# Turning the filter round with plain products into 64-row halves: one change to a long-convolution and mixer kernel

## The chip, the cores and the metric

The kernel runs on one core of one Trainium2 chip. The time is the device time of one execution in microseconds, and the profile is one execution recorded by the hardware profiler. The engines are TensorE (PE, with its weight loads as PEld), VectorE (DVE), ScalarE (ACT), GpSimd (POOL) and SyncE (SP), whose queue issues nearly all transfers.

## The reference

Two branches read the same input `q` (2048 tokens of 640 channels, bf16) and are mixed by a gate per token:

```
g = sigmoid((q * gate_w).sum(-1))
# branch A: a gated long convolution
k_shift[t] = sum over 4 taps of k[t - j] * shift_k[:, j]
kv = k_shift * v
y  = causal convolution of kv with ssm_k (640 x 2048), by FFTs of length 4096, + kv * ssm_D
a  = q * y
# branch B: a mixer block
h  = gelu(layernorm(q) @ w1); its four channel quarters shifted by +1, -1, +2, -2 tokens; hs = h @ w2
x1 = q + hs
b  = x1 + gelu(layernorm(x1) @ w3) @ w4
out = g * a + (1 - g) * b
```

## The kernel before

**The layout.** A token is n*32 + g*16 + s. The row (partition) of a tile is 64*g + n, and the sixteen values of s are sixteen slots of the free dimension. All loads of `q`, `k` and `v` come in this way: rows 0 to 63 hold g = 0, rows 64 to 127 hold g = 1. This is called the signal's row order here.

**Branch B.** The normalised input is transposed on PE in pairs of slots (`tr1`, L609; copied out by `ev1` and, for the ends, `evh`), multiplied by `w1` with the shifts (`w1`, L689 and L693), put through gelu (`g1`, ACT L706), multiplied by `w2` (`w2`, L715) and added to `q` (`x1`, DVE L722). The second norm (`nm2`) and a transposing DMA (`dt2`, L808) lead to `w3` (L817), gelu (`g2`, ACT L824) and `w4` (L833, L842).

**Branch A.** The convolution is an FFT in two steps of products with tables of sines (`TRIG`). `kv` is made on DVE in four groups of eight instructions (L878, L882, L886). Step 1 takes 16 slots of the filter (`s1h`, L911) and of the signal (`s1x`, L913), is copied out of PSUM (`e1h`, `e1x`, into FS) and written to DRAM (`wF`, L943). Step 2 (`s2`, L965) reads that back after every step 1 is written; then come a product of spectra on DVE (L980), the way back (`s3`, L993), another trip through DRAM (`wG`, `rG`), and the last step (`s4`, L1031), which meets branch B on DVE (`yq`, `ad`, `ax`, `fo`).

**The filter.** `ssm_k` is stored by channel, so it has to be turned: five blocks SK of 128 channels by 2048 times. `trh` (L859) uses PE's transposing mode, 16 blocks of 128x128 for each of the five, into a bf16 PSUM tile of 2048 columns; `evt` (L387 on ACT, L389 on DVE) copies it to HT. A transpose of columns s, s + 16, s + 32 ... puts time 16*q + s into row q, so even rows hold g = 0 and odd rows g = 1. This isn't the signal's row order. Step 1 must sum over the 64 rows of each g apart, so the kernel keeps a second table BM: zeroed on POOL (`bz`, L499), then the sines written to every other row by two DMAs (`bm`, L503). Step 1 of the filter then multiplies all 128 rows, half of them with zeros; that of the signal uses rows 0 to 63 and 64 to 127 as two separate 64-row tiles of the array.

**The order.** Everything is a list of tasks (`Plan.add`), each with the engine it may run on and an estimated duration. The string ORDER fixes the sequence and the engine of each task. `Plan.place` walks it with the estimates, only to choose buffers and the number of filler products (L255, products with zeros that keep PE running while it waits early on). The eight PSUM banks are the pool U; most tasks take a pair of banks. A bank is held until its copy has ended.

Of the kernel before, what the change touches and what calls it, by code (L numbers as in the profile page):

```python
# [12 lines left out]
BF16 = mybir.dt.bfloat16  # L13
# [24 lines left out]
41 0 23 5 29 94v 6 7 9 3 19 11 17 4 25 1 2 31 32 15 18 8 10 63v 12 13 14 26 27 87v 61a 85a 64 62 95v 104v 65v 28 42 88  # L38
86 393 24 44 96 209 43 210 55a 66v 89v 67 395 56 68a 58a 53v 54 97v 34 90a 30 399 396v 400v 57v 91 397 40 394a 93a 98
59 99v 100v 92v 60v 101 103v 143 147 16 20p 33 149 398a 102a 77a 145 79v 21 45 150 80 391 71v 72 46 22 144 148 69v  # L40
392v 82v 74a 121 39 122 450 70 78 146 107a 73v 458 35 75 451v 401p 438 37 81v 76v 439a 151 83 113v 123 36 459a 38 456
152 457a 49 84v 108 114 454 452 115v 116 125 455a 453a 110v 129 117v 446 444 126 460 118v 403 404 405 124 127 447a 162
163 406 130 128 156 157 440 105a 441a 407 159 153 154 106 160 461 47 445a 402 131 158 109a 155 442 111 132 137 443a
112a 408 161 462 466 48 138 409 463a 448 134 135 468 215p 216 449 164 140 469a 467a 119 413 141 51 221p 165 470 410 50
411 120a 166 222 223v 464 465a 167 474 471a 173 475a 174 171 217a 480 168 476 187 191 481a 482 193 477a 172 473 192
188 412 414 218 483a 478 169 195 189 170 181 415 416 417 479a 472 418 419 421 422 182 178 179 485 196 194 190 486 423
488 219a 484 225a 489a 175 220 487a 492 176 493a 136 203 424 204 494 425 490 206 498 207 495a 200 201 491a 420 426 427
# [12 lines left out]
673 681 343 684 661 682a 680a 685a 344 674 686 687a 688 629 297 645 675a 689 676v 690 677 301 692v 691a 693 345 302  # L60
# [23 lines left out]
class Plan:  # L84
# [13 lines left out]
    def add(self, name, eng, dur, fn, r=(), w=(), use=(), acq=(), rel=(), roles=(), after=(), mode=None, nbytes=0):  # L98
# [3 lines left out]
        t.kept = None  # L102
        t.acq = [(a, 1, a == "U") if isinstance(a, str) else a for a in acq]
# [43 lines left out]
    def place(self, order):  # L147
# [6 lines left out]
        mode, bw, flying, self.kept = None, 0.0, [], None  # L154
        start, end = [None] * n, [None] * n
        for i in order:
# [34 lines left out]
            else:  # L191
                d = t.dur
# [17 lines left out]
                free[e] = end[i] = at + d  # L210
            for (o, p, k) in t.rel:
# [143 lines left out]
def build(env, nc, io):  # L355
    pl = Plan()
    add = pl.add
    for name, n in (("U", 8), ("xn", 4), ("hs", 2), ("x1nT0", 1), ("x1nT1", 1), ("h2", 2), ("FS", 2), ("FX", 5), ("XS", 2), ("HS", 2), ("PP", 2),
                    ("GX", 4), ("Q", 2), ("O", 2), ("V", 4)):
# [51 lines left out]
    add("ident", "POOL", 0.55, c_id, r=["iotb"], w=["ID"])  # L411
# [92 lines left out]
    add("bm", "SP", 1.08, c_bm, r=["TRIG"], w=["BM"], nbytes=P * 4096 * HALF, roles=("C0",))  # L504

# [6 lines left out]
    add("cjp", {"POOL": 3.2, "ACT": 2.3}, 0, lambda t: copy(t, env["VC"][0:1, 3, :, :],  # L512
# [106 lines left out]
    for s0 in pairs:  # L619
        nm = []  # L620
        for s in (s0, s0 + 1):
            st1[s] = add(f"st1.{s}", {"DVE": 1.26, "ACT": 1.73}, 0, lambda t, s=s: f_st1(t, s), r=[("x", s, 0), ("x", s, 1)],
                         w=[("MV", s)])
            add(f"rs1.{s}", "POOL", 0.85, lambda t, s=s: f_rs1(t, s), r=[("MV", s), "c0"], w=[("RS", s)])
        for s in (s0, s0 + 1):
# [7 lines left out]
            nm1[s] = add(f"nm1.{s}", {"DVE": 0.445, "ACT": 1.2}, 0, f_nm1, r=[("RS", s), ("x", s, 0), ("x", s, 1)],  # L633
# [10 lines left out]
        def f_ev1(t, s0=s0, tt=tt):  # L644
            copy(t, env["xnT"][:, s0 + 2:s0 + 4, :, :], tview(env.Ub(tt.buf["U"][0])))
        add(f"ev1.{s0}", {"ACT": 1.25, "DVE": 0.82}, 0, f_ev1, use=[tt], rel=[(tt, "U")], w=[("xnT", s0), ("xnT", s0 + 1)],
            roles=("xnT",))
        if s0 in (14, 0):
            h0 = 0 if s0 == 14 else 18

            def f_evh(t, s0=s0, tt=tt, h0=h0):
# [10 lines left out]
            add(f"evh.{s0}", {"DVE": 1.0, "ACT": 1.3}, 0, f_evh, use=[tt], rel=[(tt, "U")], w=[("xnT", a), ("xnT", a + 1)],  # L662
                roles=("xnT",))
# [130 lines left out]
    for c in range(4):  # L794
        nT, nP = None, f"x1nT{c % 2}"
        for s0 in (4 * c, 4 * c + 2):
            ss = (s0, s0 + 1)
            add(f"ve2.{s0}", {"DVE": 0.42, "POOL": 1.5}, 0, lambda t, s0=s0: f_ve2(t, s0), r=[("x", s, 0) for s in ss] + [("S2", s) for s in ss],
                w=[("v2", s0)])
            add(f"st2.{s0}", "POOL", 1.5, lambda t, s0=s0: f_st2(t, s0), r=[("v2", s0)] + [("x", s, 0) for s in ss],  # L800
# [53 lines left out]
    for cb in range(5):  # L854
        def trh(t, cb=cb):
            sk = env["SK"][:, cb, :].rearrange("c (q s) -> c q s", s=16)
            o = env.Ub(t.buf["U"][0])
            for i in range(16):
                nc.tensor.transpose(o[:, 128 * i:128 * i + 128], sk[:, :, i], env["ID"][:])  # L859
        t = add(f"trh.{cb}", "PE", 1.0, trh, r=["ID", ("SK", cb)], use=[fill], acq=("U",), mode="f", roles=("SK",))  # L860

        def evt(t_, cb=cb, t=t):
            copy(t_, env["HT"][:, :, 128 * cb:128 * cb + 128], env.Ub(t.buf["U"][0]).rearrange("p (s c) -> p s c", s=16))
        add(f"evt.{cb}", {"ACT": 1.86, "DVE": 1.23}, 0, evt, use=[t], rel=[(t, "U")], w=[("HT", cb)], after=("PRE",), roles=("HT",))
    add("dfold", {"DVE": 0.5, "POOL": 0.9}, 0, lambda t: (nc.vector if t.on == "DVE" else nc.gpsimd).tensor_tensor(out=env["HT"][0:1, 0, :], in0=env["HT"][0:1, 0, :],
                                                               in1=env.early("DR", [1, D], BF16), op=ALU.add),
        r=["DR"] + [("HT", cb) for cb in range(5)], w=["HT0"], roles=("HT", "C0"))
# [33 lines left out]
    def step1(which, order):  # L901
# [3 lines left out]
        def reads(s, cbs):  # L905
            return ["BM" if which == "h" else "TRIG"] + ([("HT", cb) for cb in cbs] + (["HT0"] if s == 0 else []) if which == "h" else [("kv", s)])
        roles = ("HT", "C0") if which == "h" else ("K",)

        def prod(out, s, c0, c1, g):
            if which == "h":  # L910
                nc.tensor.matmul(out, lhsT=BM()[:, g, 128 * s:128 * s + 128], rhs=src(s)[:, c0:c1], start=True, stop=True)  # L911
            else:
# [194 lines left out]
```

## Time and profile before

| what | value |
|---|---|
| time, median of 3 runs (lowest to highest) | 225.08 us (224.55 to 225.7) |
| the profiled execution: time, span | 227.05 us, 225.3 us |
| busy PE, DVE, ACT, POOL | 212.7, 189.3, 154.4, 45.8 us |
| instructions | 5381 |
| moved by DMA | 57.94 MB, mean 257 GB/s |
| granted TensorE clock | 1.000 |

The profiled execution's own time is 1.97 us above the median of the runs, and its span is 1.75 us below its time. Busy PE contains the filler products. Shares over the whole span hide the stages: up to about 40 us PE waits for loads, norms and copies; from then on it is nearly always at work.

### The profile page before, as it was taken

What the parts mean: (1) busy time and instruction counts of PE and PEld (TensorE: products, weight loads), DVE (VectorE), ACT (ScalarE), POOL (GpSimd) and SP (SyncE); (2) the same over time, 40 slices, a digit from 0 to 9 for tenths busy, and PEclk for the clock granted to TensorE, in tenths of its full rate; (3) what the DMA queues carried; (4) which work ended last, traced back from release to release, by engine and by line L of the source; (5) the groups of instructions that cost most, each with busy time, mean ns of one, the idle gap of its engine ahead of it and who ended that gap; (6) DMA issues with size and microseconds to landing.
All of it is one profiled execution on the core that took longest, in us unless ns stands there. A gap on an engine that the chain in (4) does not pass through costs nothing.

```text
span 225.3 us, 5381 instructions
## 1 busy us (share of the span) xinstructions
PE 212.7 (94%) x2161; PEld 106.4 (47%) x2178; DVE 189.3 (84%) x281; ACT 154.4 (69%) x225; POOL 45.8 (20%) x86
## 2 busy tenths in 40 slices
PE   3999889899999999999999999999999999999992
PEld 1576454466444444345543433334444555555561
DVE  7998896999999999997469989899857426989984
ACT  6998969799988999889658988888675002225000
POOL 7481532436200009930710000000000000000000
PEclk9999999999999999999999999999999999999999
DMA  6999999999999998979899989999992596988624
GB/s 193 281 308 232 220 237 238 327 233 327 349 240 287 241 272 252 379 270 270 193 367 311 373 154 285 316 304 309 247 255 88 185 374 209 281 250 249 203 64 116
DMA packets 39503, 57.94 MB, mean 257 GB/s; under 512 B 15027, under 2 KB 30645, under 8 KB 39478
## 3 DMA queue, kind: packets, MB, share of 16 engines
q1 hardware_dynamic: 39158, 57.27, 89.9%
q10 hardware_dynamic: 320, 0.33, 0.5%
q8 instruction: 17, 0.28, 0.5%
q14 instruction: 8, 0.07, 0.1%
HBM read 35.56 MB, written 18.36 MB: 239 GB/s over the span
## 4 chain that ended last, share of the span: by engine, by line
PE 63%; DMA 17%; DVE 12%; SPq 3%; issue 2%; ACT 1%; DVEq 0%
PE PS L817 18%; PE PS L833 17%; PE PS L715 9%; DMA x<-in_A_q_dram 7%; PE PS L965 5%; DMA W<-in_B_w_dram 4%; PE PS L689 4%; PE PS L993 4%; DMA SK<-in_A_ssm_k_dram 3%; DVE VC L878 3%; DVE VC L882 3%; DMA QO<-in_A_q_dram 2%; SPq L382 2%; PE PS L911 2%; PE PS L1031 1%
## 5 line engine op out<-in xcount | busy, mean ns | idle before, releaser
L824 ACT ACTIVATE h2T<-PS 128x512 bf16<-128x512 f32 x48 | 27.9, 605 | 27.3 <-PE PS L817 26.9
L833 PE MATMUL PS<-W,h2T 128*128 128x512 bf16 (+3 forms) x306 | 39.8, 298 | 0.3
L387 ACT CAST FS<-PS 128x1024 bf16<-128x1024 f32 x37 | 36.0, 1021 | 5.4 <-PE PS L913 3.5
L817 PEld LDWEIGHTS <-W 128*128 128x128 bf16 (+1 forms) x300 | 22.1, 103 | 29.4 <-issue 8.4
L833 PEld LDWEIGHTS <-h2T 128*128 128x128 bf16 (+1 forms) x312 | 22.4, 100 | 18.5 <-issue 1.6
L387 ACT CAST XH<-PS 128x1024 bf16<-128x1024 f32 x26 | 25.5, 1020 | 7.5 <-PE PS L965 7.4
L817 PE MATMUL PS<-x1nT,W 128*128 128x512 bf16 x120 | 28.5, 380 | 0.0
L817 PE MATMUL PS<-XB,W 128*64 128x512 bf16 (+1 forms) x180 | 28.5, 380 | 0.0
L980 DVE TENSOR_TENSOR PP<-XH 128x2048 bf16<-128x2048 bf16 x20 | 23.6, 1219 | 3.1 <-ACT XH L387 2.8
L878 DVE TENSOR_TENSOR VC<-K,VC 128x2560 bf16<-128x2560 bf16 x16 | 23.7, 1490 | 2.3 <-DMA W<-in_B_w_dram 2.1
L715 PE MATMUL PS<-W,hsT 128*128 128x128 bf16 (+1 forms) x155 | 23.5, 297 | 0.9 <-DMA W<-in_B_w_dram 0.6
L850 DVE TENSOR_TENSOR x<-PS,x 128x640 bf16<-128x640 f32 x12 | 9.8, 823 | 13.4 <-PE PS L833 13.2
L689 PE MATMUL PS<-xnT,W 128*128 128x512 bf16 x80 | 19.2, 379 | 0.1
L715 PEld LDWEIGHTS <-hsT 128*128 128x128 bf16 x160 | 12.8, 98 | 13.0 <-issue 1.1
L882 DVE TENSOR_TENSOR VC<-VC 128x2560 bf16<-128x2560 bf16 x12 | 17.9, 1489 | 0.3
L389 DVE CAST XH<-PS 128x1024 bf16<-128x1024 f32 x14 | 16.9, 1220 | 1.2 <-PE PS L965 1.1
L1037 DVE SCALAR_TENSOR_TENSOR W<-PS,GG,QO 128x640 bf16<-128x640 f32 x16 | 13.6, 877 | 2.4 <-PE PS L1031 1.9
L387 ACT CAST GS<-PS 128x1024 bf16<-128x1024 f32 x12 | 12.0, 1016 | 3.9 <-PE PS L993 3.9
L255 PE MATMUL PS<-C 128*128 128x512 bf16 x34 | 9.9, 434 | 3.8 <-DVE C L506 3.7
L842 PE MATMUL PS<-W,h2T 128*64 128x512 bf16 (+1 forms) x192 | 13.4, 299 | 0.0
L722 DVE SCALAR_TENSOR_TENSOR x<-PS,x 128x640 bf16<-128x640 f32 x16 | 12.8, 815 | 0.1
L965 PE MATMUL PS<-FX,TRIG 64*32 64x512 bf16 x320 | 12.4, 381 | 0.3 <-ACT GS L387 0.3
(115 smaller groups left out, 294.0 us busy)
## 6 DMA issues: line engine op xcount, KB each, us to landing
FH<-FS SPq DMA_DIRECT2D x8, 640.0 KB, 6.3
FXD<-FS SPq DMA_DIRECT2D x8, 640.0 KB, 5.0
FX<-FH SPq DMA_DIRECT2D x10, 512.0 KB, 6.0
FX<-FXD SPq DMA_DIRECT2D x10, 512.0 KB, 5.3
GX<-GD SPq DMA_DIRECT2D x8, 640.0 KB, 5.9
W<-in_B_w_dram SPq DMA_DIRECT2D x2, 1920.0 KB, 11.9
GD<-GS SPq DMA_DIRECT2D x8, 480.0 KB, 4.0
SK<-in_A_ssm_k_dram SPq DMA_DIRECT2D x5, 512.0 KB, 6.5
```

The lines of the kernel that those rows point to most:

```text
L387: nc.scalar.copy(out=out, in_=in_)
L389: (nc.vector if t.on == "DVE" else nc.gpsimd).tensor_copy(out=out, in_=in_)
L689: nc.tensor.matmul(m[:, b, :], lhsT=W[:, 0, kb, 160 * fb:160 * fb + 128], rhs=rhs(kb, shifts[fb]), start=(kb == 0), stop=(kb == 4))
L715: nc.tensor.matmul(m[:, c0:c1], lhsT=env["hsT"][:, o.buf["hs"][0], fb, 128 * (s % 4):128 * (s % 4) + 128], rhs=env["W12"][:, 1, fb, c0:c1] ...
L817: nc.tensor.matmul(env.PS[q:q + w, t.buf["U"][0], :], lhsT=env["W3"][:, kb, 128 * fb + q:128 * fb + q + w], rhs=env.nT(int(nP[-1]))[:, :, ...
L824: nc.scalar.activation(out=env["h2T"][:, o.buf["h2"][0], fb, :], in_=env.PS[:, t.buf["U"][0], :], func=ACT.Gelu_apprx_tanh)
L833: nc.tensor.matmul(m[q:q + w, c0:c1], lhsT=env["h2T"][:, o.buf["h2"][0], fb, a:a + w], rhs=env["W4"][:, fb, c0:c1], start=(fb == 0), stop= ...
L878: nc.vector.tensor_tensor(out=VC[:, o], in0=env["K"][:, a + 3 - j:a + 7 - j, :], in1=w, op=ALU.mult)
L882: nc.vector.tensor_tensor(out=VC[:, 1], in0=VC[:, 1], in1=VC[:, 2], op=ALU.add)
L965: nc.tensor.matmul(env.U(t.buf["U"][0])[32 * j:32 * j + 32, gp, :], lhsT=CRI()[64 * gp:64 * gp + 64, 32 * pc:32 * pc + 32], rhs=X[64 * gp: ...
L980: nc.vector.tensor_tensor(out=env["PP"][:, o.buf["PP"][0], a, :].rearrange("p (b c) -> p b c", b=2), in0=X.unsqueeze(1).broadcast_to([P, 2 ...
L1037: nc.vector.scalar_tensor_tensor(out=u, in0=env.Uf(t.buf["U"][0])[:, 0:D], scalar=SS("GG")[:, s:s + 1], in1=env["QO"][:, 2 * q.buf["Q"][0] ...
```

## The change

The filter is no longer transposed in PE's transposing mode but by plain products: each block of 128 channels by 64 times (of one g) is the stationary operand, the unit matrix the moving one, and the result goes to rows 0 to 63 or 64 to 127 of PSUM, so HT has the signal's row order. The result is f32, so a pair of banks holds 8 slots instead of 16: ten `trh` and ten `evt` tasks in place of five. The table BM goes, with its memset and its two DMAs, and step 1 of the filter uses the same 64-row products as the signal's. Tasks read HT by channel block and half of the slots.

The estimates of some tasks are changed as well, two one-buffer pools (T0, T14) keep `ev1` and `evh` of the same PSUM tile from overlapping in the plan, and the plan delays some DVE tasks while POOL does `cjp` or `dfold`. With these a new ORDER is given, which rearranges all engines and the SP queue.

```diff
@@ ORDER: all lines replaced (778 tasks before, 786 after, two of them gone and ten new)
@@ Plan.add, Plan.close, Plan.place
+        t.lock, t.hold = False, False
+    LOCKS = ("nm1.", "nm2.", "kv", "pa.", "pb.", "pc.", "ad.", "ax.", "phase1", "phand", "phsmall")
+        for t in self.tasks:
+            t.lock, t.hold = t.name.startswith(self.LOCKS), t.name in ("cjp", "dfold")
+                if t.lock and e == "DVE" and held[0] <= at < held[1]:
+                    start[i] = at = held[1]
@@ build
-    BM = lambda: env.early("BM", [P, 2, 2048], BF16)
-    add("bz", "POOL", 1.9, lambda t: nc.gpsimd.memset(BM().rearrange("p g q -> p (g q)").bitcast(F32), 0.0), r=["ID"], w=["BM"], roles=("C0",))
-    def c_bm(t):
-        for g in range(2):
-            nc.sync.dma_start(out=BM()[g::2, g, :], in_=env["TRIG"][64 * g:64 * g + 64, 0:2048])
...
-            for i in range(16):
-                nc.tensor.transpose(o[:, 128 * i:128 * i + 128], sk[:, :, i], env["ID"][:])
+    for cb, h in [(cb, h) for cb in range(5) for h in range(2)]:
+        def trh(t, cb=cb, h=h):
+            sk = env["SK"][:, cb, :].rearrange("c (n g s) -> c g n s", g=2, s=16)
+            o = env.Uf(t.buf["U"][0])
+            for i in range(8):
+                for g in range(2):
+                    nc.tensor.matmul(o[64 * g:64 * g + 64, 128 * i:128 * i + 128], lhsT=sk[:, g, :, 8 * h + i], rhs=env["ID"][:],
+                                     start=True, stop=True)
...
-        add(f"evt.{cb}", {"ACT": 1.86, "DVE": 1.23}, 0, evt, use=[t], rel=[(t, "U")], w=[("HT", cb)], after=("PRE",), roles=("HT",))
+        add(f"evt.{cb}.{h}", {"ACT": 1.03, "DVE": 1.23}, 0, evt, use=[t], rel=[(t, "U")], w=[("HT", cb, h)], after=("PRE",), roles=("HT",))
...
         def prod(out, s, c0, c1, g):
-            if which == "h":
-                nc.tensor.matmul(out, lhsT=BM()[:, g, 128 * s:128 * s + 128], rhs=src(s)[:, c0:c1], start=True, stop=True)
-            else:
-                nc.tensor.matmul(out, lhsT=B()[64 * g:64 * g + 64, s, :], rhs=src(s)[64 * g:64 * g + 64, c0:c1], start=True, stop=True)
+            nc.tensor.matmul(out, lhsT=B()[64 * g:64 * g + 64, s, :], rhs=src(s)[64 * g:64 * g + 64, c0:c1], start=True, stop=True)
```

In the new order the loads of `q` come first, then `w1`, then the filter, then `w2`, ahead of `k`; before, the first block of the filter came first and all of `w2` came behind the first half of `k`. PE does all of the first group of `w1` (and one part of the next) before the first `trh`, and the ten `trh` nearly in one run. Seven `evt` run on ACT and three on DVE (before: two and three). The gate's DVE work now stands among the `kv` instructions, where it stood behind them, and the copy `bperm` is on ACT, where it was on DVE.

More of the change, by code (lines that the diff above doesn't have):

```diff
@@ L43 @@
[L43 to L47, printed above, removed]
@@ L153, in place @@
         relleft, relat = dict(self.nrel), {}
-        mode, bw, flying, self.kept = None, 0.0, [], None
+        mode, bw, flying, self.kept, held = None, 0.0, [], None, (0.0, 0.0)
         start, end = [None] * n, [None] * n
@@ L210, in place @@
                 free[e] = end[i] = at + d
+                if t.hold and e == "POOL":
+                    held = (at, end[i])
             for (o, p, k) in t.rel:
@@ L410, in c_id @@
                                 channel_multiplier=1)
-    add("ident", "POOL", 0.55, c_id, r=["iotb"], w=["ID"])
+    add("ident", "POOL", 0.75, c_id, r=["iotb"], w=["ID"])
     def c_ones(t):
@@ L511, in build @@
                                                   in_=io["sk"].rearrange("d j -> (d j)").unsqueeze(0)), w=["CJR"], roles=("VC",))
-    add("cjp", {"POOL": 3.2, "ACT": 2.3}, 0, lambda t: copy(t, env["VC"][0:1, 3, :, :],
+    add("cjp", {"POOL": 2.6, "ACT": 2.3}, 0, lambda t: copy(t, env["VC"][0:1, 3, :, :],
                                                             env["VC"][0:1, 2, :, :].rearrange("p a b -> p (a b)").rearrange("p (d j) -> p j d", j=4)),
@@ L621, in build @@
         for s in (s0, s0 + 1):
-            st1[s] = add(f"st1.{s}", {"DVE": 1.26, "ACT": 1.73}, 0, lambda t, s=s: f_st1(t, s), r=[("x", s, 0), ("x", s, 1)],
+            st1[s] = add(f"st1.{s}", {"DVE": 1.37, "ACT": 1.7}, 0, lambda t, s=s: f_st1(t, s), r=[("x", s, 0), ("x", s, 1)],
                          w=[("MV", s)])
@@ L632, in f_nm1 @@
                                             scalar2=SS("RS")[:, c], op0=ALU.add, op1=ALU.mult)
-            nm1[s] = add(f"nm1.{s}", {"DVE": 0.445, "ACT": 1.2}, 0, f_nm1, r=[("RS", s), ("x", s, 0), ("x", s, 1)],
+            nm1[s] = add(f"nm1.{s}", {"DVE": 0.445, "ACT": 0.95}, 0, f_nm1, r=[("RS", s), ("x", s, 0), ("x", s, 1)],
                          acq=("xn",))
@@ L645, in f_ev1 @@
             copy(t, env["xnT"][:, s0 + 2:s0 + 4, :, :], tview(env.Ub(tt.buf["U"][0])))
-        add(f"ev1.{s0}", {"ACT": 1.25, "DVE": 0.82}, 0, f_ev1, use=[tt], rel=[(tt, "U")], w=[("xnT", s0), ("xnT", s0 + 1)],
-            roles=("xnT",))
+        e1 = add(f"ev1.{s0}", {"ACT": 1.25, "DVE": 0.82}, 0, f_ev1, use=[tt], rel=[(tt, "U")], w=[("xnT", s0), ("xnT", s0 + 1)],
+                 roles=("xnT",), acq=(f"T{s0}",) if s0 in (14, 0) else ())
         if s0 in (14, 0):
@@ L661, in build @@
             a = -2 if s0 == 14 else 16
-            add(f"evh.{s0}", {"DVE": 1.0, "ACT": 1.3}, 0, f_evh, use=[tt], rel=[(tt, "U")], w=[("xnT", a), ("xnT", a + 1)],
-                roles=("xnT",))
+            eh = add(f"evh.{s0}", {"DVE": 0.9, "ACT": 1.3}, 0, f_evh, use=[tt], rel=[(tt, "U")], w=[("xnT", a), ("xnT", a + 1)],
+                     roles=("xnT",), acq=(f"T{s0}",))
+            for o in (e1, eh):
+                o.rel.append((o, f"T{s0}", None))
             add(f"evz.{s0}", {"POOL": 0.15, "DVE": 0.07}, 0, lambda t, z=(0, h0) if s0 == 14 else (127, h0):
@@ L797, in build @@
             ss = (s0, s0 + 1)
-            add(f"ve2.{s0}", {"DVE": 0.42, "POOL": 1.5}, 0, lambda t, s0=s0: f_ve2(t, s0), r=[("x", s, 0) for s in ss] + [("S2", s) for s in ss],
+            add(f"ve2.{s0}", {"DVE": 0.42, "POOL": 1.8}, 0, lambda t, s0=s0: f_ve2(t, s0), r=[("x", s, 0) for s in ss] + [("S2", s) for s in ss],
                 w=[("v2", s0)])
-            add(f"st2.{s0}", "POOL", 1.5, lambda t, s0=s0: f_st2(t, s0), r=[("v2", s0)] + [("x", s, 0) for s in ss],
+            add(f"st2.{s0}", "POOL", 2.0, lambda t, s0=s0: f_st2(t, s0), r=[("v2", s0)] + [("x", s, 0) for s in ss],
                 w=[("r2", s) for s in ss])
@@ L851, in build, with evt @@
             add(f"t2.{s}", "DVE", 0.83, t2, use=[t], rel=[(t, "U")], w=[("x", s, 0), ("x", s, 1)])
[L854 to L857, printed above, removed]
-            for i in range(16):
[L859 to L863, printed above, removed]
-        add(f"evt.{cb}", {"ACT": 1.86, "DVE": 1.23}, 0, evt, use=[t], rel=[(t, "U")], w=[("HT", cb)], after=("PRE",), roles=("HT",))
-    add("dfold", {"DVE": 0.5, "POOL": 0.9}, 0, lambda t: (nc.vector if t.on == "DVE" else nc.gpsimd).tensor_tensor(out=env["HT"][0:1, 0, :], in0=env["HT"][0:1, 0, :],
+    for cb, h in [(cb, h) for cb in range(5) for h in range(2)]:
[6 more added lines that the diff above has]
+                                     start=True, stop=True)
+        t = add(f"trh.{cb}.{h}", "PE", 0.5, trh, r=["ID", ("SK", cb)], use=[fill], acq=("U",), mode="c64", roles=("SK",))
+        def evt(t_, cb=cb, h=h, t=t):
+            copy(t_, env["HT"][:, 8 * h:8 * h + 8, 128 * cb:128 * cb + 128], env.Uf(t.buf["U"][0]).rearrange("p (s c) -> p s c", s=8))
+        add(f"evt.{cb}.{h}", {"ACT": 1.03, "DVE": 1.23}, 0, evt, use=[t], rel=[(t, "U")], w=[("HT", cb, h)], after=("PRE",), roles=("HT",))
+    add("dfold", {"DVE": 0.5, "POOL": 1.5}, 0, lambda t: (nc.vector if t.on == "DVE" else nc.gpsimd).tensor_tensor(out=env["HT"][0:1, 0, :], in0=env["HT"][0:1, 0, :],
                                                                in1=env.early("DR", [1, D], BF16), op=ALU.add),
-        r=["DR"] + [("HT", cb) for cb in range(5)], w=["HT0"], roles=("HT", "C0"))
+        r=["DR"] + [("HT", cb, 0) for cb in range(5)], w=["HT0"], roles=("HT", "C0"))
     for gi in (3, 2, 1, 0):
@@ L905, in reads @@
         def reads(s, cbs):
[L906 to L907 removed]
+            return ["TRIG"] + ([("HT", cb, s // 8) for cb in cbs] + (["HT0"] if s == 0 else []) if which == "h" else [("kv", s)])
+        roles = ("HT",) if which == "h" else ("K",)
         def prod(out, s, c0, c1, g):
[L910 to L914 removed]
+            nc.tensor.matmul(out, lhsT=B()[64 * g:64 * g + 64, s, :], rhs=src(s)[64 * g:64 * g + 64, c0:c1], start=True, stop=True)
+        mode, dur, durr = "r64", 0.23, 0.28
         for a in order:
```

23 lines of the change are left out of this document (2 added, 21 removed), and 5 rows, old and new, of the table ORDER.

## The prediction

> **What bounds the kernel now.** I read the table of stages first (each engine's busy time in stretches of 10 us), because the 94% of PE over the span mixes stages. Columns: stretch, length, then busy us and instructions of PE, PEld, DVE, ACT and POOL, the granted clock, the DMA share, GB/s.
>
> ```profile
> 0.00:10.00 10.00, 6.27 (x39) 3.19 (x40) 8.37 (x33) 7.86 (x13) 5.98 (x23) 1.00 0.75 233
> 10.00:20.00 10.00, 9.56 (x105) 7.10 (x106) 9.68 (x27) 9.81 (x13) 6.66 (x11) 1.00 1.02 277
> 20.00:30.00 10.00, 8.38 (x62) 4.47 (x61) 8.18 (x22) 7.87 (x13) 4.13 (x7) 1.00 1.02 227
> 30.00:40.00 10.00, 9.46 (x90) 4.40 (x88) 7.72 (x19) 8.94 (x14) 2.00 (x4) 1.00 0.97 246
> ...
> 90.00:100.00 10.00, 9.89 (x60) 4.11 (x60) 9.69 (x14) 8.67 (x14) 7.46 (x6) 1.00 0.90 318
> ```
>
> Then the chain that ended last, in order of time (start, us, what):
>
> ```profile
> 30.95 9.63 DMA W<-in_B_w_dram
> 40.58 0.05 issue
> 40.63 1.75 PE PS L715 x11
> ...
> 48.45 0.56 PE PS L609 x10
> ...
> 50.37 0.86 PE PS L911 x4
> ...
> 52.59 0.43 PE PS L911 x2
> ...
> 54.94 1.08 PE PS L689 x5
> ...
> 63.81 0.45 PE PS L911 x8
> ...
> 71.94 0.54 PE PS L913 x4
> ...
> 73.94 0.32 PE PS L913 x2
> ...
> 75.73 0.55 PE PS L913 x10
> ...
> 96.30 1.49 DVE K L886
> ...
> 101.33 6.84 PE PS L833 x49
> ...
> 193.49 3.26 PE PS L833 x48
> ```
>
> And the costliest groups, with shapes kept apart (busy us, mean ns of one, idle before):
>
> ```profile
> L387 ACT CAST FS<-PS 128x1024 bf16<-128x1024 f32 x37 | 36.0, 1021 | 5.4 <-PE PS L913 3.5 <-PE PS L911 1.6 <-PE PS L689 0.2
> L722 DVE SCALAR_TENSOR_TENSOR x<-PS,x 128x640 bf16<-128x640 f32 x16 | 12.8, 815 | 0.1
> L255 PE MATMUL PS<-C 128*128 128x512 bf16 x34 | 9.9, 434 | 3.8 <-DVE C L506 3.7
> L859 PE MATMUL PS<-ID,SK 128*128 128x128 bf16 x80 | 5.9, 227 | 1.0 <-DMA SK<-in_A_ssm_k_dram 0.6 <-DVE HT L389 0.3
> L387 ACT COPY HT<-PS 128x2048 bf16<-128x2048 bf16 x2 | 3.7, 1855 | 0.0
> L389 DVE COPY HT<-PS 128x2048 bf16<-128x2048 bf16 x3 | 3.7, 1221 | 0.7 <-PE PS L859 0.7
> L389 DVE CAST FS<-PS 128x1024 bf16<-128x1024 f32 x3 | 3.6, 1212 | 0.0
> ```
>
> The reader is to see two stages. From 40.63 us, when `w2` has landed and its first product (L715) runs, the chain is mostly PE without gaps. So the end is the moment at which PE's unbroken run begins, plus the work that is left then. Before that, PE was busy 6.27 + 9.56 + 8.38 + 9.46 = 33.7 us in 40, of which 9.9 are fillers (L255): 23.8 us of useful work, and 40.6 - 23.8 = 16.8 us lost. DVE is nearly as full: up to the last write of `kv` (L886 at 96.30) it sits on the chain, so a gain of PE before 101 us counts only as far as DVE follows.
>
> **The change part by part.**
>
> *Step 1 of the filter (on PE's path).* A pair of 512-column products on all rows takes 0.43 us (L911 x2), the eight 128-column ones of four slots 0.45. Before: 16 x 0.43 + 4 x 0.45 = 8.7 us. The signal's same products as 64-row tiles are in the trace: two slots 0.54, one slot 0.32, one slot with the eight short ones 0.55. So a slot costs about 0.22, the eight short ones 0.22, and each visit another 0.10 for the change of tile shape. The new order has 13 visits: 16 x 0.22 + 4 x 0.22 + 13 x 0.10 = 5.7 us. Gain 3.0 us; bounds 4.3 (no cost per visit) and 2.4 (every slot alone at 0.32, the short ones 0.28).
>
> The Trainium skill, TensorEngine Tiling (Array Packing), Key Properties, says that changing the tiling mode drains TensorE. The trace agrees, with 0.10 us per visit; by that rule and by the rows the sum is the same 5.7, and without it 4.4.
>
> *Turning the filter.* 160 products of 128 columns in place of 80, in column halves that may overlap. `w4` in such halves gives the price: 24 of 512 and 24 of 128 columns in 3.26 us, where a full-width 512 takes 0.216 (L689 x5 in 1.08) and a 128 takes 0.056 (L609 x10 in 0.56). 12 pairs of both are 12 x 0.272 = 3.26, so halves overlap fully. 80 pairs at 0.056 are 4.5 us, against 5.2 before:
>
> ```profile
> 13.68 0.81 PE L255 MATMUL PS<-C 128*128 128x512 bf16 x3
> 14.33 1.17 PE L859 MATMUL PS<-ID,SK 128*128 128x128 bf16 x16
> 15.33 0.81 PE L255 MATMUL PS<-C 128*128 128x512 bf16 x3
> ```
>
> (16 in 1.0 us from start to the filler behind them, 65 ns each; the weights are read with a stride). Bounds: 4.5 (full overlap), 10.4 (160 at 65 ns, none). I take 5.2, no change, since the stride stays; PE waits for copies there anyhow.
>
> *Copies of the turned filter.* Seven on ACT at 1.02 (nearest row: same shape, FS, f32) are 7.1 us against 2 x 1.86 = 3.7: ACT gets 3.4 us more. Three on DVE at 1.21 against three at 1.22: nothing. Whether this costs is a matter of the start, next.
>
> *The table BM.* Its memset (POOL, beside everything) and two SP issues go, with 0.5 MB read and written. At 246 GB/s the transfer is 2 us, in the stage where the DMA engines are full (share 0.97 to 1.02). It brings `w2` and `k` forward; it is no separate term.
>
> *The new order up to the first `w2`.* `w2` is issued ahead of `k`. The issues by size (KB each, us to landing):
>
> ```profile
> SK<-in_A_ssm_k_dram SPq DMA_DIRECT2D x5, 512.0 KB, 6.5
> ...
> W<-in_B_w_dram SPq DMA_DIRECT2D x1, 800.0 KB
> ...
> W<-in_B_w_dram SPq DMA_DIRECT2D x1, 640.0 KB, 9.6
> ```
>
> It stands behind `q` (2048 x 640 bf16, 2.6 MB), `w1` (0.8) and the filter (2.6), and is 0.8 MB itself (640 KB and four of 40): 6.8 MB at about 235 GB/s, the mean of the first three stages being 246, is 29 us, against 40.58 now. But then copies are last. ACT's queue, with its present paces:
>
> ```profile
> 4.68 2.56 ACT L483 ACTIVATE TRIG<-PRE,C 128x1024 bf16<-128x1024 f32 x3
> 7.15 0.72 ACT L585 ACTIVATE JK<-x 128x640 bf16<-128x640 bf16 x1
> ...
> 8.95 0.74 ACT L585 ACTIVATE JK<-x 128x640 bf16<-128x640 bf16 x1
> ...
> 24.26 1.28 ACT L706 ACT_TABLE_LOAD   x1
> 25.55 1.57 ACT L706 ACTIVATE hsT<-PS 128x512 bf16<-128x512 f32 x3
> ...
> 35.01 2.85 ACT L387 CAST FS<-PS 128x1024 bf16<-128x1024 f32 x3
> ```
>
> After: one sine ends at 5.75; six statistics at 1.80 (7.15 to 8.95) to 16.55; two sines (1.5) to 18.1; table load to 19.3; one gelu (0.52) 19.9; two statistics 23.5; five gelus 26.1; seven copies at 0.95 to 32.7. Three copies run beside them on DVE. Four pairs of banks hold ten `trh`, one `tr1` and the first `w2`, the twelfth user: it needs the eighth release, and by then ACT has given four or five, DVE three or four (the `tr1`'s among them): about 31 to 32 us. I take 31.5. PE's useful work by then: five `tr1` (2.8), six parts of `w1` at 1.08 to 1.19 (6.7), `trh` (5.2), small ones 0.2: 14.9 us. Lost: 16.6 us, against 16.8. So the start is neutral; bounds -2.5 (`w2` at 29) and +5 (below).
>
> Other moves. POOL builds the unit matrix behind three norms, around 11 us; the first `tr1` waits for it, beside fillers. SP issues `q` 0.46 us earlier, without the filter's first block ahead. `bperm` on ACT costs about 1.9 (as the 2048-wide HT copy) where ACT has slack (8.67 of 10 busy); if that cover is gone, it delays one norm's input by 1.9 us, not PE directly.
>
> *DVE up to the last `kv`.* From the first `kv` instruction to the last write:
>
> ```profile
> 38.45 2.89 DVE L878 TENSOR_TENSOR VC<-K,VC 128x2560 bf16<-128x2560 bf16 x2 [2.06 <-DMA W<-in_B_w_dram]
> ```
>
> this takes 59.3 us now (38.45 to 97.79): 32 x 1.49 = 47.7, fifteen `x1` at some 0.8, one norm 0.44. In the new order eleven `x1` stand there (-3.2), no norm (-0.4), and the gate's work comes in (+1.4): -2.2 us if `kv` starts at the same 38.5. By the sums above `w2` has delivered three `x1` by then, as the order asks, and `k`, behind `w2` but with BM gone, lands no later.
>
> **The sum.** PE alone: -3.0 - 0.2 = -3.2 us. DVE allows -2.2 at the last `kv`; behind it the gate no longer stands ahead of FS copies (1.4) but two `x1` do (1.6). I take the mean, -2.7, at the start of `w4` (101.33 now). From there on the work is the same set, so the profiled span 225.3 becomes 222.6, its time 224.3, and against the median of 225.08 (1.97 lower than the profiled execution) **222.4 us**, 1.2% faster. A half per cent, 1.1 us, is about what the runs here can tell from no change.
>
> **The rivals.**
> *The copies hold PE at the start (slower).* ACT gains 3.4 us of copies and five gelus, each holding a bank, stand ahead of them. If the first `w2` comes at 36.5, 5 us more are lost and the time is 222.4 + 5 = 227.4. It decides from 34.2 on, where the gain of 2.7 is used up. For it: ACT and DVE were 9.81 and 9.68 busy of 10 in the stage from 10 us. Against it: both idle about 2 us in the next (8.18 and 7.87). 16%. The Trainium skill, TensorEngine Tiling (Array Packing), PSUM Bottleneck, warns of this: tiling speeds up TensorE but not emptying PSUM. No row here shows ten such copies in a run.
> *DVE is the bound.* If `k` lands 1.7 us later, the DVE stretch gives only -0.5: 224.6. For it: the 2.06 us wait for DMA at 38.45. Against it: less is moved. 12%.
> *The halves don't overlap* in the filter's step 1: 16 x 0.43 again, gain 0 or less, 225.1. Against it stand all L913 rows. 2%.
> *The start is better too.* `w2` at 29: 222.4 - 2.5 = 219.9. 15%.
> *My forecast*, -2.7 with about 1.3 either way (221.1 to 223.7): 55%.
>
> **The numbers.** The range from 219.6 to 226.0 leaves out half of the slower rival and a small part of the best one. Faster by over 0.5%: 55 + 15 + a part of DVE's, 73%; within it 10%; slower 17%.
>
> **What would show it.** A visit of two filter slots at 0.54 and about 5.7 us for step 1 show the first term. The first `w2` at 31 to 32 us, led by copies to HT and not by DMA, shows the start. The last `kv` write ending near 95.5 and the first `w4` near 98.6 show DVE's term. The forecast is wrong if PE idles or fills longer before `w2`, if PE gets gaps between 35 and 95 us, or if the reads of step 2 come no earlier, so that PE waits behind `w4`.

## The result, and the profile after

The changed kernel takes 230.37 us (median of 5 runs, 229.91 to 230.58) against 225.01 (5 runs): 1.0234 times as long, 95% interval 1.0212 to 1.0257. It is slower, and the forecast of 222.4 with its range up to 226.0 was wrong in sign. The profiled execution took 230.51 us with a span of 228.5.

The kernel before takes 224.4 to 226.5 us in most executions and up to 228.4 in some; its profiled one, at 227.05, was one of the slower, while that of the changed kernel is at its median.

The groups of the changed kernel that answer to the turning (weight load, product, ACT's copy; busy us, mean ns, idle before):

```profile
L836 PEld LDWEIGHTS <-SK 128*64 128x64 bf16 x160 | 9.0, 204 | 0.5 <-DMA SK<-in_A_ssm_k_dram 0.4
L836 PE MATMUL PS<-ID,SK 128*64 128x128 bf16 x160 | 9.3, 276 | 0.0
L369 ACT CAST HT<-PS 128x1024 bf16<-128x1024 f32 x7 | 6.9, 1014 | 3.4 <-PE PS L836 3.4
```

The chain of the changed kernel (start, us, what). L836 is the turning, L691 `w2`, L888 step 1, L809 `w4`, L940 step 2:

```profile
24.47 1.24 PE PS L665 x5
25.71 8.15 PE PS L836 x144
33.85 0.67 PE PS L583 x10
34.52 1.04 PE PS L836 x16
35.55 1.47 PE PS L691 x10
37.02 0.54 PE PS L888 x4
...
42.06 0.32 PE PS L888 x2
...
48.58 0.33 PE PS L888 x8
...
102.74 6.64 PE PS L809 x48
...
113.13 6.89 DMA FX<-FXD
```

The turning stands on the chain in nearly one run, 8.15 + 1.04 = 9.2 us, 57 ns for each load of 64 columns, and nothing hides it. ACT's copies waited 3.4 us for PE, not PE for them. The first `w2` starts at 35.5.

VectorE's timeline of the changed kernel (start, us, line, shapes) at the first `kv` and at the last:

```profile
41.71 0.82 DVE L698 SCALAR_TENSOR_TENSOR x<-PS,x 128x640 bf16<-128x640 f32 x1
42.45 1.49 DVE L856 TENSOR_TENSOR VC<-K,VC 128x2560 bf16<-128x2560 bf16 x1
...
98.18 1.49 DVE L864 TENSOR_TENSOR K<-VC 128x2560 bf16<-128x2560 bf16 x1
```

The first `kv` stands behind the third `x1` (L698) on DVE, which needs the third part of `w2`. It starts at 42.45, where it was 38.45 before; the last ends at 99.67 (97.79 before).

The third place is behind `w4`. PE's timeline and SP's of the changed kernel, then the same two of the kernel before:

```profile
102.67 13.21 PE L809 MATMUL PS<-W,h2T 128*128 128x512 bf16 x96
116.46 0.63 PE L940 MATMUL PS<-FX,TRIG 64*32 64x512 bf16 x16 [0.57 <-DMA FX<-FH]
...
120.06 0.41 PE L940 MATMUL PS<-FX,TRIG 64*32 64x512 bf16 x8 [1.20 <-DMA FX<-FXD]
```

```profile
105.61 6.38 SPq L784 DMA_TRANSPOSE XB<-xn  x3
112.17 0.45 SPq L932 DMA_DIRECT2D FX<-FH  x1
```

```profile
101.26 13.21 PE L833 MATMUL PS<-W,h2T 128*128 128x512 bf16 x95
114.40 0.62 PE L965 MATMUL PS<-FX,TRIG 64*32 64x512 bf16 x16
```

```profile
103.96 5.65 SPq L808 DMA_TRANSPOSE XB<-xn  x3
109.78 0.45 SPq L957 DMA_DIRECT2D FX<-FH  x1
```

Before, the first read of step 2 was issued 8.5 us behind the start of `w4` and was there when `w4` ended, 13.1 us behind its start. After, it is issued 9.5 us behind, and PE waits 0.57 and 1.20 us. Two stages of the changed kernel (columns as in the prediction) show PE early, at a lower clock, and the gap behind `w4`:

```profile
10.00:20.00 10.00, 8.37 (x61) 4.88 (x61) 7.21 (x22) 9.58 (x20) 6.99 (x13) 0.83 1.03 265
...
110.00:120.00 10.00, 8.29 (x83) 3.98 (x80) 5.15 (x7) 6.67 (x9) 2.93 (x11) 1.00 1.01 266
```

In the first, PE ran 61 instructions (105 before, the turning among them) and the granted clock was 0.83: ten products of `tr1`, 0.72 us at 10.9 us, took 1.27 at 13.3. The lower clock didn't set the first `w2`: experiment 4 has the same 0.83 in this stage, and its `w2` starts at 31.64.

### The profile page after: what moved, and what is told of

It is laid out like the page before. It is cut to its first block, busy times and chain, and to the rows that moved or that the text cites. A ratio compares the mean times of both kernels' runs of the same rounds, so it can differ in the third digit from the quotient of the medians.

```text
span 228.5 us, 5553 instructions
## 1 busy us (share of the span) xinstructions
PE 218.0 (95%) x2259; PEld 108.2 (47%) x2259; DVE 187.4 (82%) x273; ACT 158.9 (70%) x233; POOL 44.8 (20%) x89
## 4 chain that ended last, share of the span: by engine, by line
PE 82%; DMA 8%; SPq 4%; DVE 3%; ACT 1%; issue 1%; ACTq 0%
PE PS L793 23%; PE PS L809 15%; PE PS L691 10%; PE PS L665 6%; PE PS L818 6%; PE PS L888 5%; DMA x<-in_A_q_dram 5%; PE PS L968 5%; PE PS L940 5%; PE PS L836 4%; DMA FX<-FXD 3%; PE PS L1006 2%; SPq L364 2%; PE PS L669 2%; PE PS L583 1%
## 5 line engine op out<-in xcount | busy, mean ns | idle before, releaser
L809 PE MATMUL PS<-W,h2T 128*128 128x512 bf16 (+3 forms) x312 | 40.3, 299 | 0.0
L369 ACT CAST FS<-PS 128x1024 bf16<-128x1024 f32 x38 | 37.2, 1020 | 2.6 <-PE PS L888 1.9
L809 PEld LDWEIGHTS <-h2T 128*128 128x128 bf16 (+1 forms) x312 | 22.4, 100 | 18.6 <-issue 1.7
L793 PE MATMUL PS<-x1nT,W 128*128 128x512 bf16 x120 | 29.3, 380 | 0.1
L369 ACT CAST XH<-PS 128x1024 bf16<-128x1024 f32 x24 | 23.8, 1014 | 7.2 <-PE PS L940 7.1
L691 PE MATMUL PS<-W,hsT 128*128 128x512 bf16 (+1 forms) x160 | 24.1, 299 | 0.0
L371 DVE CAST XH<-PS 128x1024 bf16<-128x1024 f32 x16 | 19.6, 1223 | 3.6 <-PE PS L940 3.1
L691 PEld LDWEIGHTS <-hsT 128*128 128x128 bf16 x160 | 12.8, 98 | 12.8 <-issue 1.9
L369 ACT CAST GS<-PS 128x1024 bf16<-128x1024 f32 x14 | 13.9, 1016 | 4.3 <-PE PS L968 4.3
L940 PE MATMUL PS<-FX,TRIG 64*32 64x512 bf16 x320 | 12.9, 382 | 1.8 <-DMA FX<-FXD 1.2
L698 DVE SCALAR_TENSOR_TENSOR x<-PS,x 128x640 bf16<-128x640 f32 x16 | 12.9, 820 | 1.3 <-PE PS L691 1.1
L237 PE MATMUL PS<-C 128*128 128x512 bf16 x37 | 11.5, 469 | 1.6 <-DVE C L480 1.6
```

Source lines behind the costliest of these rows:

```text
L369: nc.scalar.copy(out=out, in_=in_)
L371: (nc.vector if t.on == "DVE" else nc.gpsimd).tensor_copy(out=out, in_=in_)
L691: nc.tensor.matmul(m[:, c0:c1], lhsT=env["hsT"][:, o.buf["hs"][0], fb, 128 * (s % 4):128 * (s % 4) + 128], rhs=env["W12"][:, 1, fb, c0:c1] ...
L793: nc.tensor.matmul(env.PS[q:q + w, t.buf["U"][0], :], lhsT=env["W3"][:, kb, 128 * fb + q:128 * fb + q + w], rhs=env.nT(int(nP[-1]))[:, :, ...
L809: nc.tensor.matmul(m[q:q + w, c0:c1], lhsT=env["h2T"][:, o.buf["h2"][0], fb, a:a + w], rhs=env["W4"][:, fb, c0:c1], start=(fb == 0), stop= ...
L940: nc.tensor.matmul(env.U(t.buf["U"][0])[32 * j:32 * j + 32, gp, :], lhsT=CRI()[64 * gp:64 * gp + 64, 32 * pc:32 * pc + 32], rhs=X[64 * gp: ...
```

## The experiments

All ratios are to the kernel before, run beside them on the same chip.

**1. The kernel before, again.** No edit.

> The kernel before, unchanged, for a second profile: the first profiled execution was 2.0 us above the median. Both theories: 225.0 us. If the profile's span is about 223.3, the 2 us of the first profile lie in one stage, and the stages of the kernel after have to be set against this one.

225.96 us, ratio 1.0017 (0.9982 to 1.0052). Differences below a half per cent mean nothing here. Its profiled execution took 227.86 us, again about 2 above the median, with a span of 226.0, not 223.3. In this profile, too, VectorE waits 2.06 us ahead of the first `kv`, here for the taps (`shift_k`), which make a trip through the DRAM tensor CD:

```profile
39.87 2.89 DVE L878 TENSOR_TENSOR VC<-K,VC 128x2560 bf16<-128x2560 bf16 x2 [2.06 <-DMA VC<-CD]
```

The profile of experiment 2, which lies at its median, has no such wait. So the 2 us probably lie there, and the first `kv` of a median execution of the kernel before would start near 36.5 (an estimate: 225.0 less the 188.6 of the table further down). No profile of such an execution shows it.

**2. Step 1 alone, in the old order.**

```diff
-                nc.tensor.matmul(out, lhsT=BM()[:, g, ...], rhs=src(s)[:, c0:c1], ...)
+            nc.tensor.matmul(out, lhsT=B()[64 * g:64 * g + 64, s, :], rhs=src(s)[64 * g:64 * g + 64, c0:c1], ...)
-    (bz: memset of BM; bm: two DMAs)
```

> The kernel before in its own order, without the table BM, step 1 of the filter in 64-row halves; the filter is still turned in 128-wide transposes, so its rows are in the wrong order and the filter's spectrum is wrong (left out: the reordering). Only step 1 and BM change. Theory 1 (the step-1 term is right, the turning is what costs): 225.0 - 3.0 = 222.0 us, between 221 and 223. Theory 2 (DVE holds the path up to 101 us, so PE's gain is lost): 224 to 225.

224.46 us, 0.9943 (0.991 to 0.9977): 1.0 us of the 3.0 expected for it, as theory 2 had it. The profiled execution took 224.13. From the first `kv` to the last write it takes 59.7 us (35.68 to 95.36), where it took 59.3: DVE doesn't follow PE's gain there.

**3. The same, turned in 64-column halves.**

```diff
-            for i in range(16):
-                nc.tensor.transpose(o[:, 128 * i:128 * i + 128], sk[:, :, i], env["ID"][:])
+            for i in range(16):
+                for g in range(2):
+                    nc.tensor.transpose(o[64 * g:64 * g + 64, 128 * i:128 * i + 128], sk[:, g, :, i], env["ID"][:])   # stride 64 bytes
```

> As the run before it, but the filter is turned in 64-wide halves with the weights read at a stride of 64 bytes, into the right rows; bf16 transposes as before, five copies as before, same order of tasks. Theory 1 (160 loads of 57 ns do not overlap, 9.2 us in place of 5.2, on PE's path): 2 to 4 us above the run before it, 224 to 226. Theory 2 (the new order is what costs): within 0.5 us of the run before it.

229.56 us, 1.0165 (1.0104 to 1.0226), 5.1 us more than experiment 2, where 2 to 4 were expected. The group of its weight loads:

```profile
L859 PEld LDWEIGHTS <-SK 128*64 128x64 bf16 x160 | 9.5, 204 | 1.5 <-issue 1.5
```

So the halves cost 5 us in the old order too, and undo what step 1 brings five times over. They reach `kv` through DVE, whose copies to HT wait 4.5 us for the turning (0.8 in experiment 2).

**4. The changed kernel, weights of 64 neighbouring columns.**

```diff
-    lhsT=sk[:, g, :, 8 * h + i]
+    lhsT=env["SK"][:, cb, c:c + 64]     # c = 128 * (8 * h + i) + 64 * g
```

> The kernel after with one edit: the 64-wide weights of the turning are 64 neighbouring elements, not every 32nd (left out: the right order of times, so the filter is wrong). Theory 1 (the stride of the weights keeps the halves from overlapping): the turning takes 4.5 to 5 us in place of 9.2, the first w2 starts near 32 us, the time is 226.4 (225.9 to 227.4). Theory 1b (halves in this place do not overlap whatever the stride): unchanged, 230.4. Theory 2 (the new order is what costs; DVE or the copies hold the start): above 229.

229.8 us, 1.0174 (1.0098 to 1.0251). The groups of loads and of ACT's copies, then two lines of the timelines of PE and DVE, and one of the chain:

```profile
L837 PEld LDWEIGHTS <-SK 128*64 128x64 bf16 x160 | 4.6, 110 | 0.9 <-DMA SK<-in_A_ssm_k_dram 0.4 <-issue 0.3
L369 ACT CAST HT<-PS 128x1024 bf16<-128x1024 f32 x7 | 6.5, 1046 | 0.0
```

```profile
31.64 1.53 PE L691 MATMUL PS<-W,hsT 128*128 128x512 bf16 x10 [0.44 <-ACT HT L369]
```

```profile
41.06 1.49 DVE L857 TENSOR_TENSOR VC<-K,VC 128x2560 bf16<-128x2560 bf16 x1 [2.38 <-DMA K<-in_A_k_dram]
```

```profile
26.56 14.38 DMA VC<-CD
```

The first eighty loads took 2.42 us here, 30 ns each: the halves do overlap when the columns lie side by side, and `w2` starts at 31.64 behind a copy to HT, as the prediction had worked out. Yet of 3.9 us at `w2` only 0.6 us of time came by the medians, 1.4 by the ratios, whose intervals overlap; 229.8 is what theory 2 had for the time. `kv` now waits 2.38 us for its operands, and starts at 41.06. The list of waits names `k`, the chain names the read of the taps, which lands at 40.94 and which the same instruction needs.

**5. Half the stride, and 6. the halves one after the other.** In 5 the weights have a stride of 32 bytes; in 6 the two loops of the changed `trh` are exchanged.

```diff
-    lhsT=sk[:, g, :, 8 * h + i]         # rows of 32 values
+    lhsT=q[:, :, 8 * h + i]             # q: SK[:, cb, 1024 * g:1024 * g + 1024] in rows of 16 values
```

```diff
-            for i in range(8):
-                for g in range(2):
+            for g in range(2):
+                for i in range(8):
```

> The changed kernel, but each 64-wide weight is read with a stride of 16 elements (32 bytes) instead of 32 (64 bytes), so the rows of the turned filter are wrong. Stride theory: the pace of a weight load is set by the stride; 128 columns at 32 bytes took 65 ns, so 64 columns take about 33 ns, the turning 5.2 us in place of 9.2, and the first w2 starts near 31.7 us; the time is that of the kernel with neighbouring columns, 229.8 us. Rival, width theory: any strided 64-wide load takes about 57 ns and the column halves don't overlap; the turning stays at 9.2 us, w2 at 35.5, the time at 230.4.

> The changed kernel; in each trh the eight products into rows 0 to 63 come first and then the eight into rows 64 to 127, instead of in turn. If turn and turn about between the column halves is what keeps strided loads at 57 ns each, a run in one half is faster or slower by a clear amount: 30 ns each would bring w2 from 35.5 to 31.6 us. If a strided 64-wide load costs its 57 ns by itself and overlaps nothing, nothing changes: the turning 9.2 us, w2 at 35.5 us, 230.4 us.

232.15 us (1.0289, 1.0215 to 1.0363) and 232.46 us (1.0295, 1.025 to 1.034). PE's timeline of 5, then of 6:

```profile
25.21 8.90 PE L837 MATMUL PS<-ID,SK 128*64 128x128 bf16 x144
```

```profile
25.41 9.59 PE L836 MATMUL PS<-ID,SK 128*64 128x128 bf16 x144
```

That is 62 and 67 ns for each load. The theory that the stride's size sets the pace has fallen: 32 bytes are no faster than 64. Nor does the taking of turns cost anything: it saves 10 ns. In 6 the slower turning brings `w2` to 37.13, 1.6 us later. In 5 `w2` starts at 35.81 and the time is still 1.8 us above the 230.4 of the width theory; why was not traced.

**7. The fourth corner: the new order, turned by 128 columns.**

```diff
-            for i in range(8):
-                for g in range(2):
-                    nc.tensor.matmul(o[64 * g:64 * g + 64, ...], lhsT=sk[:, g, :, 8 * h + i], ...)
+            for i in range(8):
+                nc.tensor.matmul(o[:, 128 * i:128 * i + 128], lhsT=sk[:, :, 8 * h + i], ...)   # stride 32 bytes
```

> The changed kernel, turned by 80 plain products with 128-wide weights in the filter's natural order of rows (stride 32 bytes, as before the change), still into f32 and with ten copies; the rows are wrong for step 1. With the old order in both ways of turning (224.5 and 229.6) and the changed kernel (230.4) this fills the fourth corner. If the turning is the whole loss, the time falls to about 224.5. If the new order is bound by the loads of k next and by its own sequence behind w4, it stays at 229.5 to 230. The turning itself should take 80 x 65 ns = 5.2 us in either case.

228.31 us, 1.0081 (1.0027 to 1.0136), between the two times expected. Its loads, and its first `kv`:

```profile
L835 PEld LDWEIGHTS <-SK 128*128 128x128 bf16 x80 | 5.3, 148 | 0.4 <-issue 0.2
```

```profile
40.66 1.49 DVE L854 TENSOR_TENSOR VC<-K,VC 128x2560 bf16<-128x2560 bf16 x1 [2.33 <-DMA K<-in_A_k_dram]
```

A load of 128 columns at a stride takes 66 ns (5.3 us for 80), one of 64 columns at a stride 57 to 67. At a stride half the columns saved little or nothing, so 160 of them take nearly twice as long as 80. The Trainium skill, TensorE: Matmul & The Clock Gate, Weight-path perf modes, says that fast weight load is on when the number of weights is 128, about twice as fast; TensorEngine Tiling (Array Packing), Restrictions, says that column tiling disables it. The rows agree as far as a single load goes: with neighbouring columns, 64 have a mean of 110 ns (experiment 4) and 128 one of 107 (experiment 10). But this rule alone doesn't give the pace: neighbouring halves overlap and come every 30 ns, strided ones every 57. Why the stride takes the overlap away stays open.

By both ways of turning, the ratios are:

| | 128 columns | 64 columns, strided |
|---|---|---|
| old order | 0.9943 | 1.0165 |
| new order | 1.0081 | 1.0234 |

The halves cost 1.5 to 2.2 per cent in either order. The new order costs 0.7 to 1.4 more; both of its cells hold the f32 result and ten copies as well, and the 0.7 lies within the intervals.

**8. No load of the main part of `w2`** (based on experiment 4).

```diff
-    dma("ldw2a", 655360, lambda t: nc.sync.dma_start(out=env["W12"][:, 1, 0:4, :], in_=...)
+    dma("ldw2a", 655360, lambda t: nc.gpsimd.memset(env["W12"][:, 1, 0:4, :], 0.0)
```

> The new order with neighbouring columns (229.8 us), and 0.66 MB of w2 are set to zero on GpSimd instead of being loaded; the sums of w2 are therefore wrong. Theory of the loads: the first kv waited for k until 41.06 because all that stands ahead of k at about 240 GB/s has to land first; 0.66 MB less bring k 2.7 us earlier, so kv starts at about 38.7 behind the third x1, PE's wait of 1.85 us at 41.5 goes, and the last kv write ends near 95.8; the time falls by 1.3 to 2.2 us to about 228. Rival: the round trip of the taps through DRAM sets the start of kv; it stays near 41 us and the time at 229.8.

226.45 us, 1.0027 (0.998 to 1.0074): 3.35 less than experiment 4, more than the 1.3 to 2.2 expected. DVE's timeline, then PE's:

```profile
37.95 1.48 DVE L856 TENSOR_TENSOR VC<-K,VC 128x2560 bf16<-128x2560 bf16 x1
```

```profile
98.19 13.21 PE L808 MATMUL PS<-W,h2T 128*128 128x512 bf16 x94
111.63 0.62 PE L940 MATMUL PS<-FX,TRIG 64*32 64x512 bf16 x16 [0.23 <-DMA FX<-FH]
```

With 0.66 MB less in the queue the operands are in time; `kv` starts right behind the third `x1`, 3.1 us earlier. So what stands ahead of them in the queue sets the start of `kv`, and the rival fell as it was put. But the read of the taps stands behind `w2` in that queue like `k`: here it is issued at 25.70 and takes 11.2 us, where it took 14.38 in experiment 4. So experiment 8 doesn't tell `k` from the taps. In experiment 7 the wait and the chain both name `k`.

**9. The reads of step 2 ahead of one transposing DMA.**

```diff
-... 307v 261v 262 203 308 311a 542 255 ...
+... 307v 261v 542 547 262 203 308 311a 255 ...
```

> The changed kernel; the first two reads of step 2 (one of the filter, one of the signal) are issued on SP ahead of the last transposing DMA to XB instead of behind it. Theory: the reads came 9.5 us behind the first w4, where the time w4 covers them allows about 8.5; a lead of 1.5 to 2 us takes away most of PE's waits of 0.57 and 1.20 us for FX, and the time falls by 0.6 to 1.8 us from 230.4 to about 229.2. Rival: XB, now later, makes w3 wait instead, or the reads wait for the last write of step 1 in any case; no change or up to 1 us slower.

231.7 us, 1.0266 (1.0218 to 1.0315): no gain. PE's timeline:

```profile
116.51 0.62 PE L968 MATMUL PS<-FX,TRIG 64*32 64x512 bf16 x16
118.55 1.25 PE L821 MATMUL PS<-XB,W 128*128 128x512 bf16 x5 [1.41 <-DMA XB<-xn]
```

The waits for FX have gone and a wait of 1.41 us for XB has come, as the rival said. A late `kv` isn't the reason: in experiment 8 the last `kv` ends 4.5 us earlier and the first read of step 2 is still issued 9.4 us behind `w4` (107.56).

**10 to 12. Ways to have both: the filter reordered before it is turned by 128 columns** (old order, step 1 in halves, no BM). GpSimd copies each block in 10, into an order that leaves 128 neighbouring columns for each load; VectorE copies in 11, into the order g, n, s, which leaves a stride of 32 bytes; in 12 VectorE does so some places later. The edit of 11:

```diff
+    for cb in (1, 2, 4, 3, 0):
+        def rsk(t, cb=cb):
+            nc.vector.tensor_copy(out=BM()[:, SLOT[cb], :].rearrange("c (g n s) -> c n g s", g=2, s=16),
+                                  in_=env["SK"][:, cb, :].rearrange("c (n g s) -> c n g s", g=2, s=16))
```

> The old order with step 1 in 64-row halves and without the table BM, where GpSimd first copies each block of the filter into the signal's order (5 x 128x2048 bf16, about 2.1 us each by the copy of the taps, 2.54 us for 2560), and the transposes stay 80 of 128 columns, now of neighbouring columns. The result's rows are right. If the copies are hidden beside the loads and fillers, the time is that of the old order with step 1 alone, 224.5 us, 1.0 below the kernel before. Rival: the copies stand in front of the norms' small steps on GpSimd and slow DVE at the shared port; each of the five then costs up to 1 us, and the time is 225.5 to 229.

> The old order with step 1 in 64-row halves, without BM; VectorE copies each block of the filter into the order g, n, s (5 copies of 128x2048 bf16, 1.32 us each by the strided copy to XB before), and 80 transposes of 128 columns with a stride of 32 bytes turn it, 5.2 us. The rows are right. DVE gets 6.6 us of work in the first 40 us, where it idled 6.1. If that idle time takes most of it, the time is 225 to 226; if the copies stand ahead of the norms and PE waits for them, as with GpSimd (where five copies took 3.63 us each), 227 to 232.

> As the old order with the filter put into the signal's order by VectorE, but each copy and its transposes stand some places later in the order: the first behind the first tr1 instead of ahead of it, where PE waited 4.0 us for it and VectorE then 2.0 us for PE. The copies took 0.69 us each, so VectorE gets 3.4 us in all. If only the place cost the time, the first w2 comes near 38 to 41 us and the time is 224.5 to 226; if the copies hold up the norms wherever they stand, 228 to 234.

241.41 us (1.0691, 1.062 to 1.0762), 234.87 (1.0419, 1.0351 to 1.0487) and 230.19 (1.0212, 1.0145 to 1.0279). The groups of 10, then that of 11:

```profile
L1076 POOL COPY C<-SK 128x2048 bf16<-128x2048 bf16 x5 | 18.1, 3635 | 0.0
L861 PE MATMUL PS<-ID,C 128*128 128x128 bf16 x80 | 6.1, 237 | 10.7 <-POOL C L1076 10.6
L861 PEld LDWEIGHTS <-C 128*128 128x128 bf16 x80 | 5.3, 107 | 11.8 <-POOL C L1076 11.7
```

```profile
L1075 DVE COPY C<-SK 128x2048 bf16<-128x2048 bf16 x5 | 3.4, 684 | 0.0
```

Both 10 and 11 are slower than even their rivals had it (229 and 232 at most); 12 lies in the slower of its two ranges. In 10, PE waited 10.6 us for copies of 3.6 us. In 11 a copy took only 0.68 us, half of what was expected, so VectorE got 3.4 us. Moving the copies and transposes changed the time by 4.7 us: the place matters more than the copy. In 12 `kv` still starts at 41.66, 6.0 us later than in experiment 2: until then VectorE is busy 35.5 us, not 32.2, and idle 6.2 us, not 3.5, half of it waiting for PE's turning. None of the three beats the kernel before, so no version here with the rows in the right order does.

## Why the prediction was wrong

One number of the trace nearly orders these kernels: the start of the first `kv` on DVE. All times are from the profiled executions (that of 8 was the quickest of its ten runs).

| kernel | first `kv` | last `kv` ends | first `w4` | time | time less first `kv` |
|---|---|---|---|---|---|
| before | 38.45 | 97.79 | 101.26 | 227.05 | 188.6 |
| 1, before, again | 39.87 | 99.14 | 102.62 | 227.86 | 188.0 |
| 2, old order, step 1 | 35.68 | 95.36 | 98.84 | 224.13 | 188.5 |
| 3, old order, 64 columns | 40.84 | 100.92 | 104.39 | 229.97 | 189.1 |
| after | 42.45 | 99.67 | 102.67 | 230.51 | 188.1 |
| 4, neighbouring columns | 41.06 | 98.06 | 101.07 | 229.47 | 188.4 |
| 7, 128 columns | 40.66 | 97.65 | 100.66 | 228.70 | 188.0 |
| 8, no `w2` load | 37.95 | 95.18 | 98.19 | 224.60 | 186.7 |

In experiments 5, 6 and 9 to 12 the first `kv` starts between 41.66 and 52.06, and the difference is 188.0 to 189.2.

*Step 1 of the filter: its size right, its worth not.* The thirteen visits on the chain of after are 5.73 us in sum, 0.54 for two slots and 0.33 for eight short products; 5.7 was predicted. The drain at a change of tile shape is in these 5.73. Alone it moved the time by 1.0 us, not 3.0 (experiment 2).

*Turning: wrong, mis-sized by 4.0 us.* It was put at 5.2, "since the stride stays", and took 9.2. The step that failed is the inference from `w4` that column halves overlap fully. It was drawn from `w4`, half of whose products have 512 columns; here every product has 128, and the pace follows the load: 30 ns with neighbouring columns, 57 with strided ones. The upper bound of 10.4 held the truth, but it was not carried into the start. "PE waits for copies there anyhow" failed with it: ACT's copies waited 3.4 us for PE.

*Copies and the rival that they hold PE: not the cause.* Copies waited for PE. With the turning at 30 ns a load (experiment 4) they are the next bound: ACT's seven run without a gap, and PE waits 0.2 and 0.4 us for them. The rule that stood beside this rival, of the Trainium skill, TensorEngine Tiling (Array Packing), PSUM Bottleneck, that tiling speeds up TensorE but not emptying PSUM, agrees with that: a copy takes 1.05 us in experiment 4 and 1.01 in after. The rival's test, `w2` at 34.2 or later, was met (35.5), but by another cause; the size, 227.4, was short by 3.

*The start, `w2` at 31.5: wrong by 4.0, all of it the turning.* With the turning at 30 ns a load it was 31.64.

*"`k`, behind `w2` but with BM gone, lands no later": wrong.* The operands of the first `kv`, `k` and the taps, land about 41 (experiments 4 and 7), some 2.5 us later than 38.5. This was a bound of its own: with the turning mended it took over after 1.4 us (42.45 to 41.06), which is why experiment 4 gained so little. BM's transfer weighed less than the 0.8 MB of `w2` put ahead: without 0.66 MB of it they were in time (experiment 8).

*The stretch of `kv`: right.* 57.2 us against 57.1 predicted and 59.3 before. Had `kv` started at 38.5, `w4` would have started at 98.7, the 98.6 of the prediction; experiment 8 shows it, 98.19.

*"From there on the work is the same set": wrong by 2.0 us.* From `w4` to the end it is 125.8 us before and 127.8 after. In it PE waits 1.8 us for the reads of step 2; before, it waited 0.3 us, and for ACT. Experiment 8, the same order with waits of 0.4, takes 126.4, so the waits are worth about 1.4 us. The rest may be finer alternation: PE changes from line to line 73 times from `w4` on against 67, and the same 320 products of the way back are busy 11.1 us against 10.5. No run separates that. The prediction named the sign of it, reads that come no earlier, and gave it no price.

*The last step, from profile to median: wrong by 1.8.* I took 1.97 us off the profiled sum because before's profiled execution lay so far above its median. Both profiles of the kernel before lie so (1.97 and 1.90 us); the changed kernel's lies 0.14 above its median. An offset of one kernel's profile can't be taken over to another's.

The three that count add up: `w4` later by 102.67 - 98.6 = 4.1 (two causes, of which the turning alone is enough), 2.0 behind it, 1.8 for the median, 7.9 of the 8.0 us between 222.4 and 230.4. Each is read from single executions, and executions of one kernel differ by up to 4 us, so the close fit is in part luck.

## What to carry to other kernels

Price a transpose by its weight loads, by their number, width and stride, before looking at overlap; at a stride half the columns can cost as much as all of them. When two engines are full, find the instruction at which the second begins its unbroken stretch, and list everything that can hold it: the engine ahead of it, and the bytes ahead of its operands in the queue. And a reordered schedule is not "the same work" behind the change: look at how late each transfer's issue stands against the work that covers it.

## What was not expected of the hardware

A strided load of 64 columns took 57 to 67 ns at strides of 64 and of 32 bytes alike, 128 columns at 32 bytes 66 ns, and 64 neighbouring columns, taking turns between the halves, 30 ns. GpSimd's copy of 128x2048 bf16, read with a stride of 64 bytes, took 3.63 us, where 2.54 us for the taps' copy, 1x2560 with a stride of 8 bytes, had promised 2.0; the Trainium skill, GPSIMD Engine Reference, Performance pitfalls for Q7 kernels, gives half as much again for a read step above 8 bytes, and here it was 1.8 times, though the two copies differ in their rows as well. VectorE moved the same block in runs of 16 elements in 0.68 us.
